# RWKV-5 attention and a SwiGLU block on one core: two units transposed by VectorE instead of TensorE, one weight rounding moved, four weight sums moved from GpSimd to VectorE

## The chip, the core and the metric

The kernel runs on one core of one Trainium2 chip. The metric is the device time of one execution in microseconds (us); the time before is the median of three runs. The engines are TensorE (PE in the profile, with its weight loads as PEld), VectorE (DVE), ScalarE (ACT), GpSimd (POOL) and SyncE (SP), which issues most of the DMAs. ACT issues a few DMAs as well.

## The reference

There are two parts. The first is a linear attention with a decaying state, for 4 batches, 8 heads, 768 tokens and a head size of 48:

```python
for t in range(S):
    cur = np.einsum('bhd,bhe->bhde', u[None] * kt, vt)
    y[:, :, t] = np.einsum('bhd,bhde->bhe', rt, state + cur)
    state = w[None, :, :, None] * state + np.einsum('bhd,bhe->bhde', kt, vt)
```

Its output, turned to 3072 rows of 384, goes through a SwiGLU block with d_ff = 1536. The three weight matrices arrive as float64, everything else as float32:

```python
g = x @ w_gate
silu = g * (1.0 / (1.0 + np.exp(-g)))
val = x @ w_val
return (silu * val @ w_out).astype(np.float32)
```

## The kernel before, in words

**Units.** The attention is cut into 24 units of 128 token rows. Units 0 to 9 are one 128-token chunk of one batch each. From unit 10 on (`PAIRED = 10`) a unit holds two halves of 64 tokens from two batches. Inside a unit the scan over time becomes matrix products: keys and values are scaled with powers of the decay (`scale_k`, L363, and `scale_r`, L366, both on POOL, into the tile `hats`), turned so that the head dimension lies on the partitions, multiplied into a 128x128 matrix of scores per head (`scores`, L508), masked (`masked_copy`, L516, on DVE), and multiplied with the values (`outputs`, L659). `update` (L672) adds the unit to the state of its batch; L684 on DVE and L685 on POOL finish the state.

**Two ways to turn.** `turn(i)` does it on PE: four transposes of `khat` and four of `rhat` against the identity (L415, 8 matmuls) into two PSUM tiles of the ring of four, and from unit 4 on two copies by ACT into `kT` and `rT` (L419). The other way is `move_blocks(i)` and `turn_block(i, n)`: DMAs on SP move 32x32 blocks within `hats` to its last two slots (6 and 7), so that DVE, which transposes 32x32 blocks, finds each block where its transpose must land; DVE then transposes the blocks into `kT` (n = 0) and `rT` (n = 1). For the paired units these are eight DMAs (L445) and two transposes (L467). For a whole unit there is a branch with four DMAs (L429) and two transposes with a reordered access pattern (L465); before the change no unit takes it, since `BLOCKS = 10` sends units 0 to 9 to PE.

**Steps.** The program is one list in an order written out by hand: `for s in range(4, N + 2)`. Step s scales unit s+1, computes the scores of unit s-1 and the outputs of unit s-2, and loads unit s+3 (`load`, L157, and `load_v`, L163, on SP). Each engine runs its part of that list in order. `gaps(s, n)` are five places in a step, n = 0 to 4, where other work is fed in. For the steps in the table `EARLY` each letter is one piece: "F" is a piece of the feed-forward block, "R" rounds one chunk of weights.

**Feed-forward pieces.** A gate/value piece (`gate_value`, L705) is six products of a pair of units' `xT` with columns of `wgv`, into one of two PSUM banks that are used in turn; ACT applies silu to the gate half (L711), DVE multiplies by the value half (L712), and after that the bank is free for the piece after next. The output projections are L785 (`project`), later L1207, and from the third pair on the gate and value products go through L974.

**Weight rounding.** The weights come as 18 chunks of 768 KB (12 of gate and value, 6 of `w_out`): `load_weights` (L194, SP) loads a chunk of float64 bits into a ring of three tiles `w_bits`. "R" rounds a chunk: ACT scales its halves (L214, two, into PSUM banks 2 and 3) and its low words (L220), DVE puts the float32 bits together (L229 and L230, twice each), and POOL adds the rounding part (L262) when the next "R" comes. After a chunk is rounded in the list, the load of the chunk two further on is issued, into the tile of the chunk before.

**Four sums.** When all 18 chunks are rounded, an "R" stands for one call of `weight_sum` (L734) until four are done: differences of quarters of `w_out`, 128 x 1152 each, on POOL. The projections need them.

**Order around the change.** `BLOCKS` decides who turns a unit. For unit s+1 between `BLOCKS` and `PAIRED` the list has, at the end of step s, `move_blocks(s+1)` and `load_v(s+1)`, and in step s+1 `turn_block(.., 0)`, one feed-forward piece, `turn_block(.., 1)`. Units 8 and 9 use the same `rhat` slot in that case. `late` is true at even steps from `BLOCKS` on; then `scale_r(s+1)` comes after the transposes of unit s, and `load(s+3)` comes before `gaps(s, 2)` instead of after it. The line that copies `scales` (L1524) stands before `move_blocks`. `scores` puts off the second masked copy of a unit from `BLOCKS` on.

Of the kernel before, what the change touches and what calls it, by code (L numbers as in the profile page):

```python
# [22 lines left out]
def fast(  # L23
# [41 lines left out]
    dve, pool, act, pe, sp = nc.vector, nc.gpsimd, nc.scalar, nc.tensor, nc.sync  # L65
# [62 lines left out]
    def rhat_of(i):  # L128
        return rhat[i % 2 if i < BLOCKS else i % 4 // 2]

# [6 lines left out]
    PAIRED = 10  # L137
# [216 lines left out]
    def at(i, a):  # L354

        return HP - 1 - a if i >= BLOCKS and i % 2 else a

# [23 lines left out]
    def diagonal(i, on_act=None):  # L381

        du = dus.pop(i)
        if i >= PAIRED:
            small.extend(
                lambda h=h: act.activation(  # L386
                    own_of(i)[:, slot(i, h), :], ident64, AF.Identity, scale=du[:, h : h + 1]
                )
                for h in range(H)
            )  # L390
            return
        on_act = on_act or (HP if i < 4 else H)
        small.extend(
            lambda h=h: act.activation(
                At[i % 2][:, h, :], ident[:], AF.Identity, scale=du[:, h : h + 1]
            )
            for h in range(on_act)
        )
        if on_act < H:
            n = H - on_act  # L400
            pool.tensor_mul(
                At[i % 2][:, on_act:H], ident[:].unsqueeze(1).to_broadcast([P, n, P]),
                du[:, on_act:H].unsqueeze(2).to_broadcast([P, n, P]),
            )
# [4 lines left out]
    def turn(i):  # L409
        kr = khat[i % 4], rhat_of(i)  # L410
        tps = [next_psum(HP, P) for _ in kr]
        turned[i] = three.tile([P, HP, P], FP32, name="rT", tag="rT")
        for tp, t, dst, table in zip(tps, kr, (kT[i % 2], turned[i]), (pw[:, :, 1 : P + 1], pv)):
            for a in range(HP):
                pe.transpose(tp[:, a, :], pair(t, a), ident[:])  # L415
            if i < 4:
                dve.tensor_mul(dst[:], tp[:], table)
            else:
                act.copy(dst[:], tp[:])  # L419
# [79 lines left out]
    def scores(i):  # L499
# [20 lines left out]
        lazy.popleft()()  # L520
        if i < BLOCKS:
            lazy.popleft()()
# [206 lines left out]
    def weight_sum():  # L729

        n = len(summed)
        o = (wt[1][:], w12, wt[0][:], wt[2][:])[n]
        a, b = ((w22, w12), (w12, w11), (w22, w12), (w21, wt[0][:]))[n]
        pool.tensor_sub(o, a, b)  # L734
        summed.append(n)

    part_of = {}
# [585 lines left out]
    def feed(n, pops=1, lazies=1):  # L1323
        for _ in range(n):
            ready = [k for k, (need, _) in enumerate(todo) if need <= done["pool"] + len(summed)]
            if ready:
                todo.pop(ready[0])[1]()
            for _ in range(min(len(lazy), lazies + (len(lazy) > 9))):
                lazy.popleft()()
            for _ in range(min(pops, len(small))):  # L1330
                small.popleft()()
# [22 lines left out]
    def gaps(s, n):  # L1354

        if s not in EARLY:
            if n == 0:
                coming = 40 * ((s < 14) + (s < 18)) + 14 * (s < 22)
                share[0] = -(-(len(todo) + coming) // max(25 - s, 1))
            feed(  # L1360
                share[0] // 5 + (n < share[0] % 5) - (n == 1 and BLOCKS <= s < PAIRED),
                1,
            )
            return
        for what in EARLY[s][n]:
            if what == "R":
                if done["pool"] < NW:
                    round_weights()
                elif len(summed) < 4:
                    weight_sum()  # L1370
            else:
                feed(1, 3, 2)

    share = [0]
    BLOCKS = 10
    LATE = 10
    EARLY = {s: ("" if s < 7 else "R", "F", "R", "F", "RF") for s in range(5, 12)}
    EARLY[10] = ("", "FF", "RR", "F", "RF")
    EARLY[11] = ("R", "FF", "R", "F", "RF")
    EARLY[4] = ("R", "F", "", "F", "F")  # L1380

    def flush():
# [89 lines left out]
    for s in range(4, N + 2):  # L1472
        if 4 < s <= PAIRED:
            own_sum(s)
        if s == PAIRED:
            diagonal(s)
        late = BLOCKS < s + 1 < N and s % 2 == 0
        if s + 1 == BLOCKS:
            turn(s)
# [54 lines left out]
        if s + 1 == PAIRED:  # L1534

            for e in range(2):
                rows, o = slice(64 * e, 64 * e + 64), 64 - 64 * e
# [49 lines left out]
@with_exitstack  # L1587
def kernel(
    ctx: ExitStack,
    tc: tile.TileContext,  # L1590
    *args: bass.AP,
):
    nc = tc.nc
    ctx.enter_context(tc.manual_schedule())
    flag = ctx.enter_context(tc.tile_pool(name="flag", bufs=1))
    outside = flag.tile([1, 1], INT32, name="outside")
    n = fast(tc, *args, outside[:])
    with tc.If(n > 0, label="general"):
        general(tc, *args)
# [397 lines left out]
```

## Time and profile before

| what | value |
|---|---|
| median of three runs | 580.8 us (579.77, 580.8, 583.33) |
| the profiled execution | 581.99 us, of which the span is 580.3 us |
| mean granted TensorE clock | 0.996 |
| busy: PE / PEld / DVE / ACT / POOL | 569.6 / 512.9 / 427.8 / 223.3 / 393.2 us |
| DMA moved | 49.16 MB |

In the rows of a timeline the first number is the start in us from the beginning of the span, the second how long the instruction (or the merged run of equal instructions, x8) lasted. An `SPq` or `ACTq` row is a DMA being issued, not its transfer. In a row of groups, "x24 | 10.0, 415" is the count, the busy time in us and the mean of one in ns; what follows is idle time of that engine just before, and who ended it. In a row of windows, the busy time of each engine stands with its count in brackets, and the row ends with the granted clock, the busy share of the DMA engines, and GB/s. One float32 matmul of the kernel leaves two records on PE (a transpose leaves one), so a gate/value piece of six shows as x12.

### The profile page before, as it was taken

How to read it: one execution, taken by the hardware profiler on the slowest of the kernel's cores; microseconds unless marked ns; L12 is line 12 of the kernel's file. 1: busy time of each engine (PE TensorE's matmuls, PEld its weight loads, DVE VectorE, ACT ScalarE, POOL GpSimd, SP SyncE). 2: the span in 40 equal slices, each digit the busy share in tenths (PEclk: the TensorE clock that was granted, in tenths of full speed). 3: DMA queues.
4: the chain of work that ended last, by engine and by line, in shares of the span. 5: the costliest groups of instructions: out<-in, count | busy, mean ns of one | idle time of the engine just before them, and what ended most of it. 6: DMA issues, size and time to landing. Idle time of an engine off the chain costs nothing.

```text
span 580.3 us, 13714 instructions
## 1 busy us (share of the span) xinstructions
PE 569.6 (98%) x5418; PEld 512.9 (88%) x5418; DVE 427.8 (74%) x753; ACT 223.3 (38%) x532; POOL 393.2 (68%) x395
## 2 busy tenths in 40 slices
PE   8899999999999999999999999999999999999996
PEld 7688888899888899988899988899988899988896
DVE  7687887389597689497879597868268787477772
ACT  3468888422344422353521344421233320234310
POOL 6689888998999927979527979528988950010700
PEclk9899999999999999999999999999999999999999
DMA  8979986545455326535424544310200000200002
GB/s 201 233 213 246 285 231 124 94 76 111 94 88 102 68 47 124 105 73 99 71 45 89 128 72 83 56 34 20 55 1 0 1 1 2 54 2 0 2 1 59
DMA packets 152663, 49.16 MB, mean 85 GB/s; under 512 B 139729, under 2 KB 142802, under 8 KB 152594
## 3 DMA queue, kind: packets, MB, share of 16 engines
q1 hardware_dynamic: 147794, 41.22, 33.8%
q10 hardware_dynamic: 4800, 7.02, 4.4%
q8 instruction: 44, 0.72, 0.5%
q14 instruction: 25, 0.20, 0.1%
HBM read 28.31 MB, written 4.72 MB: 57 GB/s over the span
## 4 chain that ended last, share of the span: by engine, by line
PE 93%; POOL 3%; DMA 1%; DVE 1%; SPq 1%; issue 1%; ACT 0%; POOLq 0%; DVEq 0%
PE bank L974 29%; PE bank L785 18%; PE ring L974 13%; PE bank L705 12%; PE bank L1207 8%; PE ring L594 2%; PE ring L659 2%; PE ring L560 2%; POOL s L904 2%; PE ring L508 2%; PE ring L415 1%; PE ring L1207 1%; DMA hats<-in_r_dram 1%; PE ring L608 1%; SPq L445 1%; PE ring L316 1%
## 5 line engine op out<-in xcount | busy, mean ns | idle before, releaser
L998 DVE TENSOR_TENSOR hv<-hv,bank 128x512 f32<-128x512 f32 x132 | 87.6, 682 | 39.2 <-PE bank L974 34.3
L705 PE MATMUL bank<-xT,wgv 128*128 128x256 f32 x288 | 67.9, 391 | 1.7 <-POOL wgv L238 1.5
L974 PE MATMUL bank<-xf,wgv 128*128 128x256 f32 x256 | 65.8, 381 | 0.1
L705 PEld LDWEIGHTS bank<-xT,wgv 128*128 128x128 f32 x288 | 54.5, 194 | 10.3 <-POOL wgv L238 1.7
L998 ACT COPY hv<-bank 128x512 f32<-128x512 f32 x72 | 40.8, 584 | 59.0 <-PE bank L974 53.8
L974 PEld LDWEIGHTS bank<-xf,wgv 128*128 128x128 f32 x256 | 47.9, 190 | 7.2 <-DVE kT L1252 0.6
L1261 POOL TENSOR_TENSOR hv<-At,hats 128x512 f32<-128x512 f32 x8 | 10.2, 1272 | 63.8 <-ACT At L1260 63.8
L1005 ACT ACTIVATE hv<-hv 128x512 f32<-128x512 f32 (+2 forms) x36 | 22.8, 633 | 51.6 <-DVE hv L998 51.6
L974 PE MATMUL bank<-xT,wgv 128*128 128x256 f32 x144 | 35.7, 380 | 0.0
L974 PE MATMUL bank<-xT,s 128*128 128x256 f32 x152 | 35.2, 379 | 0.0
L386 ACT ACTIVATE zs<-mask,du 128x64 f32<-128x64 f32 x96 | 29.6, 346 | 12.0 <-DVE hv L798 6.1
L785 PE MATMUL bank<-wt,hs 128*128 128x192 f32 x192 | 34.1, 328 | 0.0
L785 PE MATMUL bank<-wo,hs 128*128 128x192 f32 x192 | 33.9, 327 | 0.0
L762 POOL TENSOR_TENSOR hs<-hv,hs 128x768 f32<-128x768 f32 x6 | 11.2, 1874 | 31.6 <-DVE hs L759 31.6
L974 PEld LDWEIGHTS bank<-xT,s 128*128 128x128 f32 x152 | 28.8, 190 | 4.2 <-issue 0.3
L785 PE MATMUL bank<-wo,hv 128*128 128x192 f32 x192 | 32.5, 326 | 0.0
L785 PEld LDWEIGHTS bank<-wo,hs 128*128 128x128 f32 x192 | 31.7, 190 | 0.5 <-DVE hv L793 0.3
L785 PEld LDWEIGHTS bank<-wo,hv 128*128 128x128 f32 x192 | 31.6, 190 | 0.4
L904 POOL TENSOR_TENSOR s<-s 128x256 f32<-128x256 f32 x39 | 31.4, 805 | 0.8
L785 PEld LDWEIGHTS bank<-wt,hs 128*128 128x128 f32 x192 | 31.4, 190 | 0.2
L904 POOL TENSOR_TENSOR s<-wgv 128x256 f32<-128x256 f32 x39 | 29.6, 776 | 2.6 <-PE bank L785 2.6
L627 POOL TENSOR_TENSOR v_ld<-v_ld,w 48x384 f32<-48x384 f32 x24 | 21.9, 913 | 13.5 <-DVE v_ld L624 10.3
(238 smaller groups left out, 1439.0 us busy)
## 6 DMA issues: line engine op xcount, KB each, us to landing
hats<-hats SPq DMA_DIRECT2D x112, 64.0 KB, 2.4
w_bits<-in_moe_w_gate_dram SPq DMA_DIRECT2D x6, 768.0 KB, 6.3
w_bits<-in_moe_w_val_dram SPq DMA_DIRECT2D x6, 768.0 KB
w_bits<-in_moe_w_out_dram SPq DMA_DIRECT2D x6, 768.0 KB, 6.4
At<-rT SPq DMA_DIRECT2D x28, 128.0 KB, 2.4
At<-zs ACTq DMA_DIRECT2D x24, 128.0 KB, 3.2
k_ld<-in_k_dram SPq DMA_DIRECT2D x28, 96.0 KB, 4.4
r_ld<-in_r_dram SPq DMA_DIRECT2D x28, 96.0 KB, 3.3
```

The lines of the kernel that those rows point to most:

```text
L386: lambda h=h: act.activation(own_of(i)[:, slot(i, h), :], ident64, AF.Identity, scale=du[:, h : h + 1])
L508: pe.matmul(ps[e][:, a, :], kT[i % 2][rows, at(i, a), :], turned[i][rows, at(i, a), :], start=True, stop=True, skip_group_check=True,)
L560: pe.matmul(ps[p][o : o + 64, n, :], kt[rows, n + HP * g, :], rT[rows, n + HP * g, :], start=True, stop=True, skip_group_check=True,)
L594: pe.matmul(ps[32 * q : 32 * q + 32, cc, 64 * p : 64 * p + 64], *x, start=start, stop=stop, skip_group_check=True,)
L627: pool.tensor_mul(ze, ze, w.unsqueeze(3).to_broadcast([D, HP, 2, D]))
L705: pe.matmul(gv[:, o, :].rearrange("p (i t) -> p i t", i=2), wt[:, c, P * f : P * (f + 1)], xT[:, 2 * g % NX : 2 * g % NX + 2, c, :], start ...
L785: pe.matmul(ps, lhs[:, f, :], rhs[:, f, :], start=(f == 0 and n in (0, 1, 4)), stop=(f == FH - 1), skip_group_check=True,)
L904: op(made[o], made[a], made[b])
L974: pe.matmul(ps[:, o], u[:, o], v, start=first and o == 0, stop=True, skip_group_check=True,)
L998: do(out, *(pair_of(wide[a][:]) if isinstance(a, str) else a for a in args))
L1005: todo.append((at, lambda: act.activation(gate, gate, AF.Silu)))
L1207: pe.matmul(ps, (h[what][q] if h[what] is D_ else h[what][:, q])[:, f, :], wide["o"][what][:, f, :], start=first and f == 0 and (split or ...
```

## The change

`BLOCKS` goes from 10 to 8, so units 8 and 9 are turned by DVE from moved blocks and not by PE. The table of steps 7 to 11 changes: step 7 has two roundings where it had three, steps 8 and 9 lose the "F" of gap 1 (the piece now stands between the two transposes), and step 11 has one more "R" at its start. The four sums are DVE's.

```diff
@@ weight_sum
-        pool.tensor_sub(o, a, b)
+        dve.tensor_sub(o, a, b)
@@ the table of the steps
-    BLOCKS = 10
+    BLOCKS = 8
     LATE = 10
     EARLY = {s: ("" if s < 7 else "R", "F", "R", "F", "RF") for s in range(5, 12)}
+    EARLY[7] = ("R", "F", "", "F", "RF")
+    for s in range(BLOCKS, PAIRED):
+        EARLY[s] = ("R", "", "R", "F", "RF")
     EARLY[10] = ("", "FF", "RR", "F", "RF")
-    EARLY[11] = ("R", "FF", "R", "F", "RF")
+    EARLY[11] = ("RR", "FF", "R", "F", "RF")
     EARLY[4] = ("R", "F", "", "F", "F")
```

Lines after the table have a number higher by three in the changed kernel (L1524 is L1527). On PE the order of all matmuls stays as it is, less the sixteen transposes of units 8 and 9.

The first place is SP's queue around steps 7 to 9. `w_bits_1028` is the tile of chunk 15 in the changed kernel, `w_bits_1035` that of chunk 16 before; each is the load that stands at gap 2 of step 8. `k_ld1` and `r_ld1` there are the loads of unit 11. Before:

```order
L194 DMA w_bits_961<-in_moe_w_out_dram 128x2x768
L163 DMA v_ld1_106<-in_v_dram 128x4x48 x2
L194 DMA w_bits_1003<-in_moe_w_out_dram 128x2x768
L1524 DMA scales_80<-scales_80 64x768
L194 DMA w_bits_1035<-in_moe_w_out_dram 128x2x768
L157 DMA k_ld1_104<-in_k_dram 64x8x48 x2
L157 DMA r_ld1_102<-in_r_dram 64x8x48 x2
L692 DMA v_ld2_107<-zs_100 48x4x48 x2
L194 DMA w_bits_1112<-in_moe_w_out_dram 128x2x768
```

In the changed kernel:

```order
L194 DMA w_bits_954<-in_moe_w_out_dram 128x2x768
L194 DMA w_bits_982<-in_moe_w_out_dram 128x2x768
L1527 DMA scales_80<-scales_80 64x768
L429 DMA hats_109<-hats_109 32x32x32 x4
L163 DMA v_ld1_106<-in_v_dram 128x4x48 x2
L157 DMA k_ld1_104<-in_k_dram 64x8x48 x2
L157 DMA r_ld1_102<-in_r_dram 64x8x48 x2
L194 DMA w_bits_1028<-in_moe_w_out_dram 128x2x768
L692 DMA v_ld2_107<-zs_100 48x4x48 x2
L194 DMA w_bits_1101<-in_moe_w_out_dram 128x2x768
L194 DMA w_bits_1130<-in_moe_w_out_dram 128x2x768
```

The load of a weight chunk at gap 2 of step 8 stood right behind the copy of `scales`; now four moves of unit 9's blocks, two loads of values and four loads of keys and queries stand between them. The moves write the two slots of `hats` that the transposes of unit 8 read.

The second place is ACT in step 9, up to the silu (L711) of the piece in bank 0. Before:

```order
L419 COPY kT1_113<-ring0_96 128x512
L419 COPY rT_1127<-ring1_97 128x512
L214 ACTIVATE bank2_94<-w_bits_1035 128x384
L220 ACTIVATE w_low_1145<-w_bits_1035 128x768
L214 ACTIVATE bank3_95<-w_bits_1035 128x384
L394 ACTIVATE At0_110<-ident_85,du_974 128x128 x2
L711 ACTIVATE sgs_91<-bank0_92 128x256
```

In the changed kernel:

```order
L394 ACTIVATE At0_110<-ident_85,du_967 128x128 x3
L214 ACTIVATE bank2_94<-w_bits_1028 128x384
L220 ACTIVATE w_low_1123<-w_bits_1028 128x768
L214 ACTIVATE bank3_95<-w_bits_1028 128x384
L394 ACTIVATE At0_110<-ident_85,du_967 128x128 x2
L711 ACTIVATE sgs_91<-bank0_92 128x256
```

The two copies of the PE transposes are gone; the rounding that stands there is now that of chunk 15, whose load is the one that moved back in SP's queue, and the silu stands behind it as before.

The third place is DVE in steps 9 and 10, from the masked copies of unit 8 on. Before:

```order
L516 COPY_PREDICATED At0_110<-mask_86,ring2_98 128x4x128
L516 COPY_PREDICATED At0_110<-mask_86,ring3_99 128x4x128
L712 TENSOR_TENSOR hv_90<-sgs_91,bank0_92 128x256
L229 TENSOR_SCALAR wo_88<-bank2_94 128x384
L230 SCALAR_TENSOR_TENSOR wo_88<-bank2_94,wo_88 128x384
L229 TENSOR_SCALAR wo_88<-bank3_95 128x384
L230 SCALAR_TENSOR_TENSOR wo_88<-bank3_95,wo_88 128x384
L684 TENSOR_TENSOR zs_100<-ring1_97,zs_100 48x4x48 x2
L712 TENSOR_TENSOR hv_90<-sgs_91,bank1_93 128x256
L712 TENSOR_TENSOR hv_90<-sgs_91,bank0_92 128x256
```

In the changed kernel:

```order
L516 COPY_PREDICATED At0_110<-mask_86,ring2_98 128x4x128
L465 STREAM_TRANSPOSE kT1_113<-hats_109 128x4x128
L712 TENSOR_TENSOR hv_90<-sgs_91,bank0_92 128x256
L516 COPY_PREDICATED At0_110<-mask_86,ring3_99 128x4x128
L465 STREAM_TRANSPOSE rT_1143<-hats_109 128x4x128
L229 TENSOR_SCALAR wo_88<-bank2_94 128x384
L230 SCALAR_TENSOR_TENSOR wo_88<-bank2_94,wo_88 128x384
L229 TENSOR_SCALAR wo_88<-bank3_95 128x384
L230 SCALAR_TENSOR_TENSOR wo_88<-bank3_95,wo_88 128x384
L684 TENSOR_TENSOR zs_100<-ring1_97,zs_100 48x4x48 x2
L712 TENSOR_TENSOR hv_90<-sgs_91,bank1_93 128x256
L229 TENSOR_SCALAR wo_88<-bank2_94 128x384
```

The two transposes of unit 9 stand among the masked copies of unit 8, and one more rounding (chunk 17: L229, L230, L229, L230) stands between the multiplications that free bank 1 and bank 0. The sums follow further down, among the four multiplications (L712) behind the transposes of unit 10: one behind the second of them, one behind the third, two behind the fourth.

## The prediction

> **What bounds the kernel now.** I read the page first, then the chain of work in order of time, then the timelines of ACT, DVE and SP between 60 and 107 us, where the change sits.
>
> ```profile
> span 580.3 us, 13714 instructions
> PE 569.6 (98%) x5418; PEld 512.9 (88%) x5418; DVE 427.8 (74%) x753; ACT 223.3 (38%) x532; POOL 393.2 (68%) x395
> ```
>
> PE is the bound: 569.6 of 580.3 us. The gaps that it has left are the first 20 us and the output's tail. So whatever PE no longer does comes off the time, and whatever makes PE wait is added, and nothing else counts. The chain shows the transposes that go and the stretch behind them:
>
> ```profile
> 75.20 0.87 PE ring L415 x8
> 87.34 0.87 PE ring L415 x8
> 94.11 5.38 PE bank L705 x24
> 102.60 10.56 PE bank L705 x48
> 118.59 9.75 PE bank L785 x60
> 166.10 10.07 PE bank L974 x44
> 178.48 21.78 PE bank L974 x100
> ```
>
> The first two rows are the transposes of units 8 and 9. The row at 94.11 is two gate/value pieces (2.69 us each), the row at 102.60 four (2.64 each). They alternate between two banks, so each needs the DVE multiplication of the piece before the last. The last two rows are the only other slack that I found: 44 matmuls took 10.07 us where the later pace, 21.78 / 100, makes 9.58. That 0.5 us is a wait behind POOL's and DVE's late work.
>
> **The change part by part. The transposes.** PE loses 2 x 0.87 = 1.74 us. Up to 75 us nothing on PE moves, from there it runs 0.87 ahead, from 87 on 1.74, if nothing makes it wait.
>
> **Where the turned blocks come from.** ACT and DVE in step 8:
>
> ```profile
> 76.65 0.56 ACT L419 COPY kT<-ring 128x512 f32<-128x512 f32 x1
> 77.59 0.52 ACT L214 ACTIVATE bank<-w_bits 128x384 f32<-128x384 f32 x1
> 80.46 1.41 DVE L516 COPY_PREDICATED At<-mask,ring 128x512 f32<-128x512 int32 x2
> 81.75 0.41 DVE L712 TENSOR_TENSOR hv<-sgs,bank 128x256 f32<-128x256 f32 x1
> L467 DVE STREAM_TRANSPOSE rT<-hats 128x512 f32<-128x512 f32 x14 | 9.8, 703 | 0.1
> ```
>
> Unit 8 is no difficulty: its moves are ready to issue when POOL has scaled it, a step (87.34 - 75.20 = 12.1 us) before DVE needs them. DVE reaches its transposes behind the two L516, which end at 81.87. They come 0.94 earlier (77.59 - 76.65, the two ACT copies gone from ahead of the rounding that DVE does first): 80.93. Then a transpose, L712, a transpose. The form of L465 is not in the trace; L467 moves the same 512 elements in 0.70 us, and I take that: 80.93 + 0.70 + 0.41 + 0.70 = 82.7. The bounds are 0.70 and, since L465 writes with a stride, twice that. PE reaches the scores of unit 8 at 87.34 + 0.87 - 1.74 = 86.5, so they do not wait at either bound.
>
> **What is late next.** Only at 82.7 may SP issue the moves of unit 9, because they overwrite what the second transpose reads. SP's rows price what is queued behind:
>
> ```profile
> 74.01 0.96 SPq L163 DMA_DIRECT2D v_ld<-in_v_dram  x2
> 79.39 0.36 SPq L194 DMA_DIRECT2D w_bits<-in_moe_w_out_dram  x1
> 79.84 1.29 SPq L157 DMA_DIRECT2D k_ld<-in_k_dram  x2
> 81.18 1.32 SPq L157 DMA_DIRECT2D r_ld<-in_r_dram  x2
> 86.71 0.55 SPq L194 DMA_DIRECT2D w_bits<-in_moe_w_out_dram  x1
> 105.31 5.96 SPq L445 DMA_DIRECT2D hats<-hats  x8
> ```
>
> A move costs SP 5.96 / 8 = 0.75, so four take 3.0 (an L429 moves twice the elements of an L445; bounds 0.75 and 1.5 each). Then two loads of values 0.96, four of keys and queries 1.29 + 1.32 and the gap between them, 2.66: 82.7 + 3.0 + 0.96 + 2.66 = 89.4. Only then is the load of chunk 15 issued; before, the load in that place went out at 79.39. How long it takes to land:
>
> ```profile
> DMA to landing us min/median/max: 6.0/6.3/6.8
> 89.00:90.00 1.00, 1.00 (x10) 0.80 (x8) 0.70 (x2) 1.00 (x3) 1.00 (x2) 1.00 1.00 390
> 90.00:91.00 1.00, 1.00 (x6) 0.90 (x5) 0.65 (x2) 1.00 (x2) 0.92 (x2) 1.00 0.82 293
> 91.00:92.00 1.00, 1.00 (x6) 0.62 (x4) 0.90 (x2) 1.00 (x4) 1.00 (x2) 1.00 0.60 93
> ```
>
> The first row is the landing of `w_bits` where it could be told. The load issued at 86.71 shows as the burst of 390 and 293 GB/s, most of its 768 KB, over by 91 to 92: 4.3 to 5.3 us after its issue. At 89.4 the queue holds the loads just ahead of it. I take 5.0 (bounds 4.3 and 6.3): landed at 94.4.
>
> **Who waits for it.** The rounding of chunk 15 stands on ACT where chunk 16's stood:
>
> ```profile
> 88.80 0.57 ACT L419 COPY kT<-ring 128x512 f32<-128x512 f32 x1
> 89.74 0.54 ACT L214 ACTIVATE bank<-w_bits 128x384 f32<-128x384 f32 x1
> 92.13 0.39 ACT L711 ACTIVATE sgs<-bank 128x256 f32<-128x256 f32 x1
> 92.41 0.55 ACT L214 ACTIVATE bank<-w_bits 128x384 f32<-128x384 f32 x1
> 92.63 1.39 DVE L516 COPY_PREDICATED At<-mask,ring 128x512 f32<-128x512 int32 x2
> 93.91 0.40 DVE L712 TENSOR_TENSOR hv<-sgs,bank 128x256 f32<-128x256 f32 x1
> ```
>
> Without the copies ACT gets to it at 88.80 - 0.87 = 87.9 and waits 6.5 us. Queued behind it are the silu of a gate/value piece (L711) and, behind the rounding on DVE, that piece's multiplication. From the start of L214 (89.74) to the end of L712 (94.31) it was 4.57 us. In the change one L516 and one transpose, 0.70 each, stand where the two L516 stood, so the same: the bank is free at 94.4 + 4.6 = 99.0. PE wants it for the second piece of the row at 94.11, at 94.11 + 2.69 - 1.74 = 95.06. **PE waits 3.9 us.**
>
> **A second wait.** From freeing that bank at 99.0 until it frees the one that the piece four later needs, DVE now has this to do without a pause: one L465, two L467, three L516, four L684, two L285, eight rounding instructions (L229 and L230) and three L712.
>
> ```profile
> L230 DVE SCALAR_TENSOR_TENSOR wo<-bank,wo 128x384 int32<-128x384 int32 x12 | 6.7, 557 | 0.4
> L285 DVE TENSOR_REDUCE du<-rk 128x8 f32<-128x384 f32 x24 | 13.0, 544 | 1.6 <-POOL rk L277 1.6
> L684 DVE TENSOR_TENSOR zs<-ring,zs 48x192 f32<-48x192 f32 x12 | 4.2, 352 | 2.2 <-PE ring L672 2.0
> L712 DVE TENSOR_TENSOR hv<-sgs,bank 128x256 f32<-128x256 f32 x24 | 10.0, 415 | 15.0 <-ACT sgs L711 14.9
> ```
>
> That is 0.70 (L465) + 1.4 (L467) + 3 x 0.70 (L516: the second of unit 8 and both of unit 9) + 4 x 0.35 + 2 x 0.54 + 8 x 0.56 + 3 x 0.415 = 12.4 us: 111.4. PE, started again at 99.0, gets there after 102.60 - 96.80 + 2 x 2.64 = 11.1 us, at 110.1, and waits 1.3 more. Undisturbed it would have been there at 102.60 + 5.28 - 1.74 = 106.1. So both waits together are 111.4 - 106.1 = 5.3 us, and they are set by when chunk 15 lands and by DVE's list, not by PE.
>
> **The sums.** On POOL they took
>
> ```profile
> L734 POOL TENSOR_TENSOR wt<-wo 128x1152 f32<-128x1152 f32 x2 | 5.3, 2628 | 0.1
> L757 DVE TENSOR_TENSOR hs<-hv 128x768 f32<-128x768 f32 x8 | 9.3, 1164 | 0.1
> L762 DVE TENSOR_TENSOR hs<-hv,hs 128x768 f32<-128x768 f32 x2 | 3.2, 1612 | 0.0
> ```
>
> 2.6 each. By DVE's two rows for 768 elements, 1152 cost 1152 / 768 x 1.16 to 1.61 = 1.75 to 2.4 us. They lie in DVE's pauses of some 2.2 us between the multiplications, while PE works on four pieces and then the scores and outputs of two units; I cost them at nothing. Without that cover the last two, 3.5 to 4.8 us together, would hold up the `hs` sums (L757, L759) that the first Strassen product waits for, by up to 1 us. POOL, 10.5 us lighter, can take back the 0.5 us at 166; I take 0.3, since its next work (L685) waits for DVE, which is late.
>
> The Trainium skill ("GPSIMD Engine Reference", section "1. Specifications") says that GpSimd shares its SBUF interfaces with VectorE and contends with DVE instructions that have two SBUF inputs. That speaks for the upper price, 2.4 us each, since each sum has two such inputs; the sum would then be the 1 us dearer that is named above. No row here separates contention from the instruction's own time.
>
> **The sum.** 580.3 - 1.74 + 5.3 - 0.3 = 583.6 us of span. The profiled execution took 1.7 more than its span and is 1.2 above the median of the runs shown, so I carry the difference, +3.3, to the median: 580.8 + 3.3 = **584.1 us**. The landing's bounds (4.3 and 6.3) move this from 583.4 to 585.4.
>
> **The rivals.**
>
> *The load is hidden: 578.6 us, not slower.* If chunk 15 lands by 94.4 - 5.3 = 89.1, neither wait appears, and the time is 580.8 - 1.74 - 0.5. For it speaks that the chunk issued at 86.71 was read at 92.41 without a wait, a lead of 5.7 us, and that DVE and ACT have idle time all along. The point from which it decides is SP's issue of that load: by about 84, where I get 89.4. Against it, everything ahead of it in the queue would have to shrink by more than 5 us, and 82.7 of the 89.4 stands on DVE's own order.
>
> *The moves and transposes are dearer than their kin: 587.5 us.* If an L429 holds SP for 1.5 us, the load is 3.0 later and so is all behind it; if an L465 takes 1.4, two are ahead of the moves and two in the DVE list, 2.8 more. One of the two gives about 584.1 + 3 = 587, both 590. For it: four moves of 1024 pieces of 128 bytes have no row here. Against: SP's rows for 64 and for 32 partitions differ little (1.29 and 1.49 for two).
>
> *The clock.* A wait of 3.9 us could make PE slow for a while. The trace has one case:
>
> ```profile
> 19.00:20.00 1.00, 0.51 (x1) 0.50 (x2) 0.79 (x2) 0.00 (x0) 1.00 (x2) 0.68 0.96 309
> 19.49 4.46 PE bank L705 x12
> 25.92 2.79 PE bank L705 x12
> ```
>
> After gaps of PE the granted clock fell to 0.68, and a piece took 4.46 us instead of 2.79: 1.7 us more. Here it would fall into the second wait (1.3) and leave 0.4: 584.5 us. It belongs to the forecast's case. The Trainium skill ("TensorE: Matmul & The Clock Gate", "Part 1: The HAM clock gate") says that after an idle window of about 3.4 us the clock is granted at half; the 0.68 in the row lies between half and full. By the rule in full the piece behind the wait would take up to twice its 2.69, 2.7 more, of which the second wait hides 1.3: an estimate of 585.5 us, inside the forecast's case.
>
> **How the numbers follow.** The forecast's mechanism (the chunk late, 582.3 to 586.3) gets 0.63, the hidden load 0.22, the dear moves 0.13, and 0.02 is left for others. A measurement here can tell about 1%, 5.8 us, from no change. Faster than 575.0 would need more than PE loses: 0.01. Slower than 586.6 are the dear moves and the forecast's upper edge: 0.15. Within 1%: 0.84. The range 578.3 to 587.3 takes in about two thirds of the hidden-load case, the forecast and half of the dear one. The likeliest case's own range is 582.3 to 586.3.
>
> **What would show it.** In the changed profile: no L415 after 63 us; L429 in two places, the second at about 82.7; an L194 at 89 to 90 and an ACT L214 that starts near 94, with the idle time before it put down to the DMA of `w_bits`; a pause on PE of 3 to 5 us before a gate/value piece near 95 to 99, a small one near 110; L465 at about 0.7 us; L734 on DVE at 1.75 to 2.4 us; the first L785 near 122 and no loss at 166. I am wrong if the L194 goes out before 85, if ACT does not wait at it, or if PE runs through from 80 to 120.

## The result, and the profile after

The changed kernel takes 586.67 us, median of six runs (585.91 to 587.40), the kernel before 580.68 us in the six runs beside it: a ratio of 1.0106, 95% interval 1.0087 to 1.0125. It is slower by about 1%, 2.6 us above my 584.1. That is inside the range of 578.3 to 587.3, but 0.4 us above the upper end that I gave the mechanism itself (586.3), in the stretch above 586.6 that had a chance of 0.15. Of all the runs in this document two, of e11 (836.86 and 1461.36 us), lie far off the rest and are left out of its median and its ratio. The profiled execution took 587.13 us, its span is 585.4 us. From the page of the changed kernel:

```profile
span 585.4 us, 13695 instructions
PE 568.6 (97%) x5402; PEld 511.6 (87%) x5402; DVE 436.9 (75%) x761; ACT 221.1 (38%) x528; POOL 383.7 (66%) x391
...
L705 PE MATMUL bank<-xT,wgv 128*128 128x256 f32 x288 | 68.1, 391 | 8.9 <-DVE hv L712 8.0
```

PE is busy 1.0 us less than before and yet ends 5.1 us later. The idle time in front of L705, which was 1.7 us and POOL's, is now 8.9 us, 8.0 of it behind L712 on DVE. Here is the place in the timelines of PE, SP and ACT of the changed kernel (start, duration, and in brackets the idle time just before and what ended it):

```profile
72.53 1.16 PE L508 MATMUL ring<-rT,kT 48*128 48x128 f32 x16
...
89.70 2.86 PE L705 MATMUL bank<-xT,wgv 128*128 128x256 f32 x12
100.53 4.40 PE L705 MATMUL bank<-xT,wgv 128*128 128x256 f32 x12 [7.97 <-DVE hv L712]
...
107.97 10.63 PE L705 MATMUL bank<-xT,wgv 128*128 128x256 f32 x48
```

```profile
80.68 2.87 SPq L429 DMA_DIRECT2D hats<-hats  x4
83.65 2.25 SPq L163 DMA_DIRECT2D v_ld<-in_v_dram  x2
85.95 1.37 SPq L157 DMA_DIRECT2D k_ld<-in_k_dram  x2
87.36 1.41 SPq L157 DMA_DIRECT2D r_ld<-in_r_dram  x2
88.87 0.57 SPq L194 DMA_DIRECT2D w_bits<-in_moe_w_out_dram  x1
```

```profile
95.71 0.51 ACT L214 ACTIVATE bank<-w_bits 128x384 f32<-128x384 f32 x1 [10.31 <-DMA w_bits<-in_moe_w_out_dram]
...
97.95 0.36 ACT L711 ACTIVATE sgs<-bank 128x256 f32<-128x256 f32 x1
```

The chain stands there as forecast, with a longer wait. The load of chunk 15 goes out at 88.87, behind the moves of unit 9 and six loads. ACT waits for it until 95.71, the silu of the piece in bank 0 stands behind that rounding, and PE gets the bank at 100.5. The chain of waits has the load itself as one piece:

```profile
88.87 6.76 DMA w_bits<-in_moe_w_out_dram
...
95.71 0.51 ACT bank L214
```

What follows on PE is slow at first. Windows of 2 us of the changed kernel, with the granted clock third from the end of a row:

```profile
96.00:98.00 2.00, 0.00 (x0) 0.00 (x0) 1.65 (x3) 2.00 (x6) 0.00 (x0) 0.71 0.93 372
98.00:100.00 2.00, 0.00 (x0) 0.00 (x0) 1.97 (x4) 2.00 (x6) 1.24 (x1) 0.50 0.08 28
...
102.00:104.00 2.00, 2.00 (x7) 1.62 (x6) 1.93 (x5) 1.35 (x4) 0.00 (x0) 0.58 0.20 33
104.00:106.00 2.00, 2.00 (x25) 1.50 (x27) 1.90 (x6) 1.90 (x6) 1.38 (x3) 1.00 0.63 93
```

The clock falls to a half while PE waits and stays there for about 3 us behind the wait: the piece at 100.53 took 4.40 us where the one at 89.70 took 2.86.

**Two starts.** One thing must be taken off before the two profiles are compared. They already differ at 24 us, where the programs are still the same. The profiled execution of before paused twice on PE between 17 and 19.5 and ran its first gate/value piece at half clock (the row 19.49 4.46 in the prediction); that of the changed kernel paused once:

```profile
18.49 2.86 PE L705 MATMUL bank<-xT,wgv 128*128 128x256 f32 x12 [0.73 <-POOL wgv L238]
```

So PE runs 2.6 us earlier in the changed profile from 24 to 72 us (the transposes at 62.89 in the one are at 60.29 in the other). Then come the gains: the scores at 76.00 are now at 72.53, which is 3.47 earlier, 2.6 + 0.87, and those at 88.15 at 83.80, 4.35 earlier, 2.6 + 1.74. The wait and the slow clock turn that into 5.4 us late at 107.97 (before 102.53). With the same start the change costs not 5.1 but 7.7 us between these two profiles, while the medians are 6.0 apart. The profile of e5 below, which is the kernel before with one part of the change that costs nothing, has the early start too. PE of the changed kernel is 7.7 us behind it at 107.97, and the spans (585.4 and 578.7) are 6.7 apart, since e5 loses 1.0 us at L608 near 201, where the changed kernel does not pause. So a pause of this kind can be 1.0 of the 1.7 us between 7.7 and 6.0; the rest is not settled. Two of the six runs of before (583.01 and 583.33) stand as far above the rest as the late start would put them.

### The profile page after: what moved, and what is told of

Same layout as the page of the kernel before. It is cut to its first block, busy times and chain, and to the rows that moved or that the text cites. A ratio compares the mean times of both kernels' runs of the same rounds, so it can differ in the third digit from the quotient of the medians.

```text
span 585.4 us, 13695 instructions
## 1 busy us (share of the span) xinstructions
PE 568.6 (97%) x5402; PEld 511.6 (87%) x5402; DVE 436.9 (75%) x761; ACT 221.1 (38%) x528; POOL 383.7 (66%) x391
## 4 chain that ended last, share of the span: by engine, by line
PE 89%; POOL 3%; DMA 3%; SPq 2%; DVE 1%; issue 1%; ACT 0%; DVEq 0%; POOLq 0%; ACTq 0%
PE bank L974 29%; PE bank L785 17%; PE ring L974 13%; PE bank L705 11%; PE bank L1207 8%; PE ring L594 2%; PE ring L659 2%; POOL s L904 2%; PE ring L560 2%; PE ring L508 1%; DMA hats<-in_r_dram 1%; PE ring L1207 1%; DMA w_bits<-in_moe_w_out_dram 1%; PE ring L608 1%; PE ring L415 1%
## 5 line engine op out<-in xcount | busy, mean ns | idle before, releaser
L998 DVE TENSOR_TENSOR hv<-hv,bank 128x512 f32<-128x512 f32 x132 | 87.6, 682 | 39.2 <-PE bank L974 33.9
L705 PE MATMUL bank<-xT,wgv 128*128 128x256 f32 x288 | 68.1, 391 | 8.9 <-DVE hv L712 8.0
L705 PEld LDWEIGHTS bank<-xT,wgv 128*128 128x128 f32 x288 | 54.4, 194 | 17.9 <-DVE hv L712 8.4
L998 ACT COPY hv<-bank 128x512 f32<-128x512 f32 x72 | 40.8, 584 | 58.4 <-PE bank L974 56.7
L904 POOL TENSOR_TENSOR s<-s,wgv 128x256 f32<-128x256 f32 x39 | 29.6, 758 | 2.9
```

The lines of the kernel that those rows point to most:

```text
L705: pe.matmul(gv[:, o, :].rearrange("p (i t) -> p i t", i=2), wt[:, c, P * f : P * (f + 1)], xT[:, 2 * g % NX : 2 * g % NX + 2, c, :], start ...
L904: op(made[o], made[a], made[b])
L998: do(out, *(pair_of(wide[a][:]) if isinstance(a, str) else a for a in args))
```

## The experiments

All times are medians on one chip per group; the kernel before took 579.9 us beside e1 to e4, 580.1 beside e5 to e8 and e9 to e11, 580.0 beside e12. First came four kernels that each undo or move one thing in the changed kernel.

**e1: the sums back on POOL.**

```diff
-        dve.tensor_sub(o, a, b)
+        pool.tensor_sub(o, a, b)
```

> The changed kernel with the four sums back on POOL. Theory (the late load of chunk 15 holds ACT, and through ACT the bank): the sums come after the stall and lie in DVE's pauses, so nothing changes: 586.7 us, at most 0.5 either way, and PE still waits 8.0 us for L712 with the granted clock at half behind it. Rival (DVE is too full, the sums hold up its multiplications): at least 2 us faster, 584.5 or less, and the wait at L712 shorter.

It took 589.13 us, ratio 1.0156 (1.0142 to 1.0170). The wait at L712 is there all the same, 8.6 us, so the sums are not its cause. But the time is longer than the changed kernel's (1.0106, 1.0087 to 1.0125), which neither theory expected. A second wait stands far behind the first, in PE's timeline of e1:

```profile
172.79 1.39 PE L974 MATMUL bank<-xf,wgv 128*128 128x256 f32 x4 [2.33 <-DVE hv L998]
```

POOL lost the 8 us of the stall too, and with 10.5 us of sums it had not caught up by then: its L366 starts at 162.86 (159.29 in the changed kernel), SP issues the moves that read it at 163.90 (160.32), and DVE waits 3.72 us for them (1.22) ahead of the L998 that PE needs. In the changed kernel POOL has the sums off its list, and PE does not wait here. That is what they are worth in it: 2.3 us by this wait.

**e2: three roundings in step 7 again.**

```diff
-    EARLY[7] = ("R", "F", "", "F", "RF")
-    EARLY[11] = ("RR", "FF", "R", "F", "RF")
+    EARLY[11] = ("R", "FF", "R", "F", "RF")
```

> The changed kernel with three roundings in step 7 again and one at the start of step 11, as before. Theory: the load that is late is the one issued at gap 2 of step 8 behind the moves and six loads, whichever chunk it brings (here 16), so ACT waits for it as now: 586.7 us, 585.5 to 588. Rival (the rounding that was taken out of step 7 is what makes the chunk late): the wait at L712 falls below 4 us and the time to 582 or less.

589.35 us, ratio 1.0158 (1.0141 to 1.0175): slower than expected. The long wait is unchanged, 8.22 us, now behind chunk 16, as the theory said; the rival is out. Two small waits for L712 are new (0.47 and 0.27 us), at 84 and 88, where one more rounding (four instructions) stands on DVE. With the gaps beside them PE loses 1.1 us there. The time is some 2.7 us above the changed kernel's; what makes up the rest is not settled. The profiled execution of e2 has the late start, 2.2 us behind that of the changed kernel, and its long wait is no shorter for it.

**e3: chunk 15 ahead of the moves.**

```diff
+        if s == BLOCKS:
+            load_weights()
         if BLOCKS <= s + 1 <= PAIRED:
             move_blocks(s + 1)
@@ round_second
-        load_weights()
+        if n != 13:
+            load_weights()
```

> The changed kernel with the load of chunk 15 issued ahead of the moves of unit 9 in SP's queue (right behind the copy of scales, where its tile has been free since 75.8), nothing else. Theory: ACT does not wait for chunk 15, the 8.0 us wait goes; the load of chunk 16, now the first behind moves and loads (out at about 91.2, landed at 97), is late next: its rounding holds ACT, and PE waits some 2.8 us for bank 1 at 98, the slow clock behind it 0 to 1.5: 7.7 of 9.5 us would go but for that, so about 581.3 us (580 to 583). Rival (DVE's work from 80 to 112 does not fit, whenever the chunk lands): 584 or more.

583.61 us, ratio 1.0060 (1.0046 to 1.0074), just above the expected 580 to 583. Moving one load in SP's queue takes back over two fifths of the loss. In ACT's and PE's timelines of e3 (its lines 664 and 660 are 663 and 659 elsewhere):

```profile
85.58 0.53 ACT L214 ACTIVATE bank<-w_bits 128x384 f32<-128x384 f32 x1 [0.41 <-DMA w_bits<-in_moe_w_out_dram]
...
97.93 0.51 ACT L214 ACTIVATE bank<-w_bits 128x384 f32<-128x384 f32 x1 [9.69 <-DMA w_bits<-in_moe_w_out_dram]
...
100.38 0.48 ACT L664 COPY xT<-ring 128x384 f32<-128x384 f32 x1
```

```profile
100.91 0.66 PE L660 MATMUL ring<-rT,zs 112*32 112x128 f32 x8 [4.92 <-ACT xT L664]
```

Chunk 15 is there when ACT wants it, and no wait for L712 is left in PE's list of waits. Chunk 16 is late in its place, and the copy of `xT` behind its rounding holds PE for 4.9 us, where I had 2.8 behind bank 1.

**e4: chunks 15 and 16 ahead of the moves.**

```diff
+        if s == BLOCKS:
+            gaps(s, 2)
+            load_weights()
         if BLOCKS <= s + 1 <= PAIRED:
             move_blocks(s + 1)
@@
-        gaps(s, 2)
+        if s != BLOCKS:
+            gaps(s, 2)
```

> The changed kernel with gap 2 of step 8 and one further load ahead of the moves of unit 9, so that chunks 15 and 16 are loaded before them and chunk 17 one place earlier as well. Theory: neither chunk is late, PE does not wait between 85 and 120, and what is left of the change is the 1.74 us of transposes that PE no longer does: 586.7 - 8.0 - 1.5 = 577.2 us, 576.5 to 579.5, faster than before by 0.3 to 0.7%. Rival (DVE does not fit): 584 or more, with waits for L712 as long as before.

582.49 us, ratio 1.0042 (1.0028 to 1.0055), not 577.2. The theory of the two late chunks falls here: both were early, and still PE waited three times for L712 (1.83, 0.94 and 1.74 us). The rival, a DVE that is too full, does not explain the first of them: DVE stood idle for the moves. SP and DVE of e4, whose profiled execution (586.95 us) is the slowest of its six and has the late start:

```profile
81.06 3.43 SPq L194 DMA_DIRECT2D w_bits<-in_moe_w_out_dram  x2
84.58 7.41 SPq L429 DMA_DIRECT2D hats<-hats  x4
```

```profile
96.32 1.09 DVE L465 STREAM_TRANSPOSE kT<-hats 128x512 f32<-128x512 f32 x1 [3.56 <-DMA hats<-hats]
```

SP needed 7.41 us to issue four moves (2.87 in the changed kernel), one of them 4.59, and DVE had them at 96.32. The second wait stands behind chunk 17: its load now follows the moves and goes out at 98.94, and ACT waits 5.05 us for it, until 103.96. Before the third, DVE works from 104.5 to 111.9 without a pause, behind that same chunk. What is put behind is late, whatever it is. So a new theory: the DMA engines are full here, and the moves are work for which they have no time. The next group tests it.

**e5: the sums alone.** The kernel before with `dve.tensor_sub` in the four sums.

> The kernel before with one part of the change: the four sums on VectorE, units 8 and 9 still turned by TensorE. Theory: there is no stall at 92 for POOL to fall behind in, so its 10.5 us are worth at most the 0.5 us pause at 166: 579.4 to 580.2 where the kernel before takes 579.9. Rival (the sums are worth the 2.4 us that e1 lost without them, whatever else is changed): 577.5 to 578.

580.04 us, ratio 1.0002 (0.9987 to 1.0017): nothing, as expected. The sums pay only behind a stall.

**e6: only unit 9 turned by DVE.**

```diff
-    BLOCKS = 8
+    BLOCKS = 9
```

> The changed kernel with only unit 9 turned by VectorE (BLOCKS = 9): four moves instead of eight, which need not wait for the transposes of unit 8, and the load of chunk 15 ahead of the four loads of keys and queries. PE keeps 8 transposes more than the change, 8 fewer than before. Theory (the moves' DMA time, about 6 us of all the DMA engines for a unit, is what makes the chunks late): with half of it, half the delay or less: PE waits 1 to 3 us in all behind chunk 15 or 16, 580.5 to 582.5 us. Rival (what is late is late because the moves of unit 9 wait for DVE's transposes of unit 8; without that wait nothing is): 578.8 to 579.4 us, no wait of PE between 85 and 115.

581.99 us, ratio 1.0033 (1.0021 to 1.0045). PE waited for L712 twice, 0.62 and 1.43 us. That is in the theory's window; the moves waited for nothing here and were still a burden.

**e7: the moves alone.**

```diff
+        if s in (7, 8):
+            move_blocks(s + 1)
         if BLOCKS <= s + 1 <= PAIRED:
             move_blocks(s + 1)
```

This is the kernel before, PE still turning units 8 and 9, with eight DMAs whose result nobody reads.

> The kernel before with the eight DMAs that move the blocks of units 8 and 9 added in the places where the change has them, their result used by nothing: TensorE turns both units as before. Theory (the DMA time of the moves is the price): the chunks loaded behind them land 5 us later or more, ACT waits for one of them at 89 to 96, and the time is 581 to 584. Rival (only the wait of the moves for DVE's transposes makes them a burden; here they wait for nothing): 579.5 to 580.5, no wait of ACT over 1 us.

585.39 us, ratio 1.0099 (1.0078 to 1.0120): the eight DMAs cost 5.3 us by themselves, more than expected and nearly what the whole change costs. ACT waits for both chunks behind them, and SP holds for 7.64 us:

```profile
77.21 7.64 SPq L429 DMA_DIRECT2D hats<-hats  x4
84.95 0.89 SPq L194 DMA_DIRECT2D w_bits<-in_moe_w_out_dram  x1
```

```profile
91.26 0.52 ACT L214 ACTIVATE bank<-w_bits 128x384 f32<-128x384 f32 x1 [3.38 <-DMA w_bits<-in_moe_w_out_dram]
...
97.37 0.51 ACT L214 ACTIVATE bank<-w_bits 128x384 f32<-128x384 f32 x1 [3.46 <-DMA w_bits<-in_moe_w_out_dram]
```

The chunk that went out at 84.95 was read 6.3 us later, and 6.3 us is also what such a load took before; so it is late because SP issued it late. PE waits 2.6 us in all for L712 behind the two chunks, 0.6 for `xT`, and 1.56 more for L998 at 166.57, where POOL is late as in e1.

How full the engines are shows in the DMA view of the window from 72 to 100 us (packets, MB, and the time of the packets as a share of the 16 engines). First the kernel before, then e7:

```profile
q1 hardware_dynamic: 12030, 5.14, 78.1%
```

```profile
q1 hardware_dynamic: 14961, 6.08, 101.3%
```

By the first row 22% of 28 us, 6.1 us, were free, and not all of it where it is wanted; by the second nothing is. The share counts packets that overlap more than once, so it can pass 100%. In stretches of 4 us from 72 to 92 it is 1.00 to 1.18 in e7, all the way, and 0.73 to 1.07 in the kernel before. The two rows do not price the moves, since they differ by other loads as well (2931 packets and 0.94 MB, where the moves of one unit are 4096 packets of 128 bytes and 0.52 MB). A price shows where the moves run alone, in the changed kernel from 67 to 70 us:

```profile
q1 hardware_dynamic: 2215, 0.28, 96.7%
```

2215 packets in 2.9 us of all the engines make 5.4 us for a unit's 4096, which is an estimate and little less than what was free. What no run separates is the engines from SP's queue: the moves were never issued from another queue. That SP was held because the engines were full is argued from these shares.

**e8: the changed kernel without the moves of unit 9.**

```diff
-            move_blocks(s + 1)
+            if s != BLOCKS:
+                move_blocks(s + 1)
```

> The changed kernel without the four moves of unit 9: its two transposes by VectorE then read the blocks of unit 8, so the outputs of unit 9 are not the reference's; all other work is the same. Theory: SP no longer waits for DVE and the DMA engines have 6 us less to do; the load of chunk 15 goes out at about 83 and lands at about 88.5, PE waits 0.5 to 1.5 us instead of 8.0: 578.5 to 580.5 us. Rival (DVE's longer list, with transposes of 1.1 us, keeps the bank even when the chunk is there): 582 or more, with waits for L712 over 3 us.

580.35 us, ratio 0.9999 (0.9980 to 1.0018): 6.3 us less than the changed kernel for four DMAs that are left out. The transposes by DVE and all else stayed. ACT's wait for chunk 15 is 4.17 us and PE's 1.89 for L712, with 0.77 later, a little over the expected 0.5 to 1.5: the chunk's load, out at 84.52, still stands behind the loads of unit 11.

**e9: the silu ahead of the waiting rounding.**

```diff
+    EARLY[9] = ("", "", "RR", "F", "RF")
@@
+        if s == 9:
+            gaps(s, 2)
         if BLOCKS <= s + 1 <= PAIRED:
             move_blocks(s + 1)
@@
-        gaps(s, 2)
+        if s != 9:
+            gaps(s, 2)
```

> The changed kernel with the rounding of chunk 15 moved from gap 0 of step 9 to gap 2, so behind the silu and the multiplication that free bank 0; SP's queue is the same as in the changed kernel. Theory (the bank is late only because its silu stands behind the waiting rounding in ACT's order): the 8.0 us wait for L712 goes; the next thing behind the roundings of chunks 15 and 16 is the copy of xT (L663), which PE needs some 4 us later, so PE waits about 5 there, with the slow clock behind it: 583 to 585.5 us where the change takes 586.7. Rival (the bank is late for a cause of its own, DVE's transposes): no change, 586 to 588.

585.67 us from four runs, ratio 1.0091 (1.0057 to 1.0125), a little above the expectation and not to be told from the changed kernel's 1.0106. The time decides nothing here; the profile does. The wait for L712 is gone and PE waits 4.95 us for `xT`:

```profile
100.63 0.65 PE L659 MATMUL ring<-rT,zs 112*32 112x128 f32 x8 [4.95 <-ACT xT L663]
```

That shows the link from ACT's order to the bank: with the same late chunk (issued at 88.75, read at 95.29), the bank is free in time when its silu stands ahead of the rounding.

**e10 to e12: can the order be mended?** e10 is e6 with chunk 15 ahead of the four moves (as in e3), which puts chunk 16 ahead of the keys of unit 11; e11 is the changed kernel with chunk 15 ahead of the moves and chunk 16 right behind them; e12 is e10 with the keys and queries of unit 11 behind chunk 17.

```diff
@@ e12, against e10
-        if s < PAIRED and not late:
+        if s < PAIRED and not late and s != 8:
             load(s + 3)
@@
         gaps(s, 4)
+        if s == 8:
+            load(s + 3)
```

> Only unit 9 turned by VectorE, with the loads of chunks 15 and 16 brought forward in SP's queue: chunk 15 ahead of the four moves, chunk 16 ahead of the loads of keys and queries of unit 11. Theory: the DMA engines have room for one unit's moves when they come in the order in which they are needed; neither chunk is late, PE does not wait between 85 and 115, and the 0.87 us of eight transposes is gained: 579.2 us, 578.6 to 580, against 580.1 before. Rival (the moves' 6 us of DMA time do not fit in any order): 581 or more.

> The changed kernel (both units) with chunk 15 ahead of the moves of unit 9 and chunk 16 right behind them, ahead of the loads of values, keys and queries. Theory: from 77 to 92 the DMA engines have to do chunk 15 (3.1 us), the moves (6), chunk 16 (3.1) and what is left of unit 8's loads, which is some 2 to 3 us more than the time until chunk 16 is wanted at 88: PE waits 1 to 3 us, 580 to 582 us, no gain over the kernel before. Rival (order alone decides): no wait, 578.2 to 579.

> As e10 (only unit 9 turned by VectorE, chunks 15 and 16 brought forward), and the loads of keys and queries of unit 11 now behind chunk 17 too, which in e10 was the late one (out at 92.08, read at 97.19). Theory: with the chunks in the order of their need the DMA engines catch up by 97, and the wait of 0.97 us behind chunk 17 goes; the keys of unit 11 are wanted only at about 97: 579.3 to 580.8 us, at best 0.8 us under the kernel before, which this measurement can hardly tell. Rival (there is no room for even one unit's moves): what is put last is late, here the keys of unit 11 and behind them the moves of unit 10, 581 us or more.

e10 took 581.42 us (1.0020, 1.0004 to 1.0035), e11 581.43 (1.0031, 1.0011 to 1.0051), e12 580.60 (1.0013, 1.0000 to 1.0026). In e11, as expected, both units do not fit: PE waited 1.41 and 1.74 us. e10 was slower than its theory and inside its rival's 581 or more: PE has no wait between 80 and 105, then 0.97 us behind chunk 17, the third in the row. With that one mended too, in e12, PE runs from 80 to 126 us without a wait and is 1.4 us ahead of e5 at 128, more than the 0.87. So for one unit the order can be mended in this stretch. At the end of the two spans nothing is left of it (578.9 and 578.7): e12 waits 0.8 us at 330 behind POOL (L277), ends its last matmul 0.7 us ahead of e5, and loses that in the output's tail. I did not follow either up. No version here beats the kernel before.

## Why the prediction was right, and where its sizes were off

**The mechanism** was right, step by step: SP's order puts the moves and six loads ahead of chunk 15, ACT stands before its rounding, the silu behind it frees the bank late, and PE waits at the second piece of the pair. e3 and e9 each cut one link of that chain, and the wait for L712 went both times. What I had not seen is the cause under it. I priced the moves by what SP takes to issue them (0.75 us each, and 0.72 is what the 2.87 in the row make). I put what they take of the DMA engines, some 5.4 us a unit by the row shown under e7, at nothing. e7 shows that the moves alone, without a wait for DVE and without the change, make the loads behind them late, and e4 that bringing loads forward for both units makes the moves late instead.

**The transposes that PE loses**: 0.87 and 1.74 us, as computed.

**DVE's transposes** took 1.10 us, not 0.70; my upper bound was twice 0.70:

```profile
L465 DVE STREAM_TRANSPOSE kT<-hats 128x512 f32<-128x512 f32 x2 | 2.2, 1097 | 0.0
...
L734 DVE TENSOR_TENSOR wt<-wo 128x1152 f32<-128x1152 f32 x2 | 3.5, 1743 | 0.1
```

**The issue of chunk 15's load** came at 88.87 for my 89.4, and that is luck. My times are those of a profile with the late start; in the profile of the changed kernel all stands 2.6 us earlier, and there the same sum gives 86.8. The load went out 2.1 us behind that: the moves were released at 80.65 instead of 80.1, by the two slower transposes, and from there SP took 8.2 us, not 6.7, most of the difference in the loads of values (2.25 for 0.96).

**The landing** is the term that I mis-sized most: 6.76 us by the chain of waits, above my 5.0 and above the bound of 6.3. The load I took it from went out into less traffic (a DMA share of 0.59 from 85 to 87 us) than this one (1.64 from 84 to 88 and 1.13 from 88 to 92); that this is the reason was not tested.

**The first wait** was 7.97 us for 3.9. The start has no part in that: it moves PE and the release of the moves alike, and e2, with the late start, waits 8.22. Of the 4.1 us between, 0.5 are the transposes ahead of the release, 1.5 SP's queue, 1.8 the landing and 0.2 the way from L214 to L712 (4.77 for 4.57). So the wait is twice my figure by three terms that were all too small.

**The clock** cost 1.5 us (4.40 for 2.86), close to the 1.7 that I had worked out, but it did not fall into a second wait, because there was none. DVE needed 12.1 us from freeing bank 0 (100.48) to freeing bank 1 (112.57) for my 12.4; PE came there only at 107.97 + 2 x 2.64 = 113.2. What I called the second wait and what I called the clock are one thing: whichever ends later counts. From 80 us on, waits of 1.89 us (e8) and less left the next piece at 2.83 to 2.86; two close together at the start, 0.85 and 1.46 us in the kernel before, halved the clock. The rule of the Trainium skill ("TensorE: Matmul & The Clock Gate", "Part 1: The HAM clock gate"), half the clock behind an idle window of about 3.4 us, agrees with the trace: 0.50 behind 8 us, and a price of 1.5 us, below the 2.7 that I had named as the most by that rule.

**The sums** took 1.35 to 2.13 us each for 1.75 to 2.4, and cost nothing on PE's path. The 0.3 us that I expected back at 166 did not come: PE was 5.27 us late at 166.10 and is so still behind it. Against the kernel before the sums on DVE are worth nothing (e5); within the change they are worth 2.4 us (e1), which I had not looked for.

The sums also show a price of their own. POOL and DVE of the changed kernel:

```profile
115.29 2.11 POOL L274 TENSOR_TENSOR rk<-r_ld,k_ld 128x384 f32<-128x384 f32 x1
117.48 2.00 POOL L277 TENSOR_TENSOR rk<-rk,scales 128x384 f32<-128x384 f32 x1
122.47 1.08 POOL L685 TENSOR_TENSOR zs<-zs,w 48x192 f32<-48x192 f32 x2 [2.99 <-DVE zs L684]
```

```profile
114.41 2.13 DVE L734 TENSOR_TENSOR wt<-wo 128x1152 f32<-128x1152 f32 x1
...
116.80 1.82 DVE L734 TENSOR_TENSOR wo<-wo 128x1152 f32<-128x1152 f32 x1
...
119.39 1.35 DVE L734 TENSOR_TENSOR wt<-wo 128x1152 f32<-128x1152 f32 x1
120.77 1.36 DVE L734 TENSOR_TENSOR wt<-wo,wt 128x1152 f32<-128x1152 f32 x1
```

While POOL works, a sum takes 2.13 and 1.82 us and POOL's own L274 and L277 take 2.11 and 2.00, twice the 1.02 and 1.00 that they took at 108 and 109. When POOL stands idle, the sums take 1.35, all four of them in e5. That is the contention of the Trainium skill ("GPSIMD Engine Reference", "1. Specifications"), of which the prediction said that no row showed it: it is there, and here POOL pays more of it than DVE. The kernel before had it too: POOL's L366 took 1.71 us at 121.49, beside DVE's sums of `hs`, and 1.01 at 104.28. The ends lie as if the two engines took turns: POOL's L363 at 115.32, the first sum at 116.54, L274 at 117.40, the second sum at 118.62, L277 at 119.48. That is read off the times and was not tested.

**The rivals.** The hidden load was out. Even with the four moves gone, in e8, chunk 15 went out at 84.52 and ACT waited 4.17 us for it. The dear moves were nearer than I allowed, though what was dear was not their issue on SP (0.72 us each) and only in part DVE's transposes (1.10 us).

**The sum.** PE lost 7.97 + 1.54 = 9.5 us where I had 5.3 for both waits, and the 0.3 us at 166 did not come back. That is 4.5 us more than forecast, and the medians show 2.6 of it. The rest lies mostly in the base: I started from the span of a profile with the late start (580.3 us), where e5 with the early one, the start of the changed kernel's profile, has 578.7. So the time came nearer to the forecast than its terms did.

## What to carry to other kernels

A DMA that rearranges data in small pieces has two prices: what its queue takes to issue it, and what the DMA engines take to do it. Look up how full they are in the window where it would stand before taking work off a busy engine by moving blocks; here 0.87 us of transposes a unit were bought with some 5.4 us of DMA time, in a stretch of 28 us that had 6 to spare. When a load is late and bringing it forward makes the next one late, as for both units in e3, e4 and e11, add up what the stretch has to do before reordering once more; with half the moves, in e12, the order could be mended. And where an engine waits in order, look at what stands behind the waiting instruction, and put short work that frees a buffer ahead of it.

## What the runs showed of the hardware that I had not expected

- **Issuing a DMA can take six times as long.** A move mostly costs SP 0.6 to 0.8 us, but single ones took 4.22 (e7) and 4.59 us (e4), both while weight chunks issued just before them were still coming in (253 GB/s from 80 to 84 us in e7, 329 from 84 to 88 in e4). A queue's issue time is not a constant of the instruction.
- **A transpose with a strided write** takes 1.10 us where the plain one of the same 512 elements takes 0.70.
- **Small pieces fill the DMA engines at a quarter to a half of the rate.** Windows of the changed kernel (the last two numbers are the DMA share and GB/s): when the moves of unit 8 run alone, and when chunks of weights flow.

```profile
67.00:70.00 3.00, 3.00 (x35) 2.62 (x23) 1.06 (x4) 0.43 (x1) 2.57 (x4) 1.00 1.00 98
76.00:80.00 4.00, 4.00 (x98) 3.45 (x97) 3.96 (x7) 2.60 (x7) 2.92 (x3) 1.00 0.99 357
```

The Trainium skill ("DMA: Bandwidth & Descriptors", "Why small descriptors are slow (HBM only)") has it that moves within SBUF don't suffer from small descriptors; its example is a remote DMA. Here these local ones do: at a share of 1.00 the engines carry 98 GB/s in pieces of 128 bytes, for 357 with the weights. The measurement decides. The price of a piece is no constant either: L445's moves in the kernel before, also 4096 pieces of 128 bytes, ran at 83 GB/s with a share of 0.54 from 91 to 97 us, which would be 154 at a full share.

- **The start has two forms.** In the profiles of before, e2 and e4 PE first waits 0.5 to 1.3 us for `hats` and then 1.45 to 1.46 us for `wgv`, the clock is granted at half and the first piece takes 4.46 to 4.54 us. In the others PE does not wait for `hats` there, the piece takes 2.83 to 2.86 us, and in the changed kernel all is 2.2 to 3.3 us earlier than in those three. The programs are the same up to there, so two profiles are to be set side by side at 24 us first.
